# A fused attention, mixture and mixing kernel on one Trainium2 core: six shared PSUM banks, a decode by masks, first-batch pooling on TensorE, and a new table of order keys

## The chip, the cores and the metric

The kernel runs on one NeuronCore of a Trainium2 chip. Five engines work side by side on it: TensorE (PE; its weight loads are shown as PEld), VectorE (DVE), ScalarE (ACT), GpSimd (POOL) and the queue that issues all DMAs (SP). The metric is device time in microseconds, the median of several runs of the whole program; lower is better.

## The reference

Eight batches, 576 tokens, model width 512, all in fp32. Three stages follow each other:

```python
k_p = k.reshape(B, H, 72, 8, 64).mean(axis=3)          # keys and values are pooled by eight
v_p = v.reshape(B, H, 72, 8, 64).mean(axis=3)
attn = softmax(q @ k_p.T / 8);  x = attn @ v_p         # 8 heads, joined to 512 columns
logits = x @ w_gate                                    # 4 experts, the best 2 are weighted by softmax
for e in range(4):                                     # each expert: causal attention with head size 64
    a = softmax(causal(x @ wq[e] @ (x @ wk[e]).T / 8))
    out += gate[e] * (a @ (x @ wv[e]) @ wo[e])
theta = out @ w_theta
y = w_tok_r @ (out * cos(theta)) + w_tok_i @ (out * sin(theta))
u = out + y
result = u + max(u @ w_ch, 0)
```

The weights `w_theta`, `w_tok_r`, `w_tok_i` and `w_ch` reach the kernel as 64-bit floating point words, so it makes fp32 out of two 32-bit halves itself (here called the decode).

## The kernel before

Almost every product is made from a high and a low part of each factor (`mm3`: high by high, low by high, high by low), so one logical product is three matmuls into one PSUM bank, and every result is evicted twice: ACT copies the high part, and DVE or POOL subtracts it from the value to get the low part.

**Stages.** In the first stage, per batch: keys and values are pooled (`pool_kv`), queries meet pooled keys 128 tokens at a time (`attn_half`: scores, maximum, exponential, normalisation, transposes, product with the values), then the projections to expert queries and keys (`proj_qk`, two pairs of experts `p`) and values and gate logits (`proj_v`), and the experts' causal attention (`moe`, calling `scores`, `norm`, `turn`, `heads`). The expert keys `kh` are copied by DMA to the other half of the partitions before `scores` may read them. While this runs, 26 pieces of `w_theta` and `w_tok` are decoded (`decode_to`) and put into DRAM as high and low parts; eight pieces of `w_ch` are decoded later. The second stage, per batch: `mix` makes `out`, theta, sine and cosine, and `tokens` makes the two large products and the result. The first `mix` stands beside the last batch of the first stage.

**Order.** Nothing is issued in the order written. `Plan` records every operation, gives each a key (a start and a length per part of the program in `PARTS`, lines 43 to 55, plus a shift per engine and tile name in `SHIFT`, lines 56 to 96), and `issue` lists them greedily: the operation that its own cost rules let start first, and among equals that with the lowest key. The rules are estimates in the code (`price`, `LAT`, `DMA_LAT`); the result is one fixed order for each engine and for SP, and every engine waits in that order.

**Names and lines that the change touches.** PSUM has eight banks: two named `t` for transposes, two named `acc` for accumulations, four named `s` for scores and for `mix`. `decode` (lines 687 to 704) uses three ACT instructions, two DVE instructions and one POOL product to make the value, then ACT and POOL to split it. `pool_kv` (lines 736 to 777) adds eight slices in three steps on POOL, in the first batch partly on DVE (`on`, `FIRST_DVE`, line 28); ACT writes the two halves of the block-diagonal tiles `kbd` and `vbd`. `WHOLE` (line 26) names the 128-token tiles whose exponential is taken in one ACT instruction over eight heads after a DVE addition of the maximum, instead of eight ACT instructions with a sum each. In `mix` (lines 1105 to 1153) DVE and ACT share the range reduction of theta.

```python
A.activation(s, hi_w.bitcast(F32), AF.Copy, bias=FLUSH)
V.tensor_scalar(t, hi_w, 3, 0x40000000, op0=OP.logical_shift_left, op1=OP.bitwise_xor)
V.scalar_tensor_tensor(t, lo_w, 29, t, op0=OP.logical_shift_right, op1=OP.bitwise_or)
A.activation(s, s, AF.Sign, bias=flush)
A.activation(t.bitcast(F32), t.bitcast(F32), AF.Abs)
P.tensor_tensor(s, s, t.bitcast(F32), op=OP.mult)
```

Of the kernel before, what the change touches and what calls it, by code (L numbers as in the profile page):

```python
# [20 lines left out]
S = 576  # L21
# [4 lines left out]
WHOLE = {1, 2, 3, 4}, {0}  # L26

FIRST_DVE = {"k0", "k2", "pm0", "v0", "vr", "vrb0", "w0", "w3", "w4", "w6"}
# [15 lines left out]
    "first": (-1302.83, 63.19), "kv first": (-249.24, 366.9), "attn first 0": (-2208.92, 30.55),  # L44
    "attn first 1": (-552.72, 6.54), "proj_v first 0": (-1145.19, 56.03), "proj_qk0 first 0": (-185.37, 1302.94),
# [3 lines left out]
    "moe1": (29.54, 22.32), "decode": (150.23, 0.58), "wp": (-141.08, 3.51), "loadc first": (-6.04, 1083.14),  # L49
    "wtok first": (-212.16, 3987.86), "moe1 last": (27.48, 103.73), "mix first": (770.4, 161.1),  # L50
    "wtok": (2281.89, 4299.31), "wch": (-794.95, 122.81), "loadc": (-901.73, 22508671.56), "tokens": (85.02, 33.36),
    "mix": (85.18, 31.94), "constants first": (-1492.94, 5143.97), "clear first": (-2169.17, 8594480.35),
    "weights first": (-1120.91, 244.57), "load 1": (-21.92, 2656.27), "load first k": (-1565.62, 16.63),
    "load first q": (-1211.16, 0.84), "load first v": (-1596.57, 239.37),
}
SHIFT = {
    "ACT.G": 310.7, "ACT.G*": -60.8, "ACT.chs": 547.28, "ACT.d_hi": 469.68, "ACT.d_raw": -47.45, "ACT.d_s": 807.39,
    "ACT.gates": 299.94, "ACT.gates*": 299.58, "ACT.kbd": -11.49, "ACT.kbd*": -340.09, "ACT.kh": -2.28,
    "ACT.kh*": 65.35, "ACT.pa": -42.54, "ACT.pa*": 44.32, "ACT.pev": 4.6, "ACT.pev*": -912.36, "ACT.pod": -26.03,
# [137 lines left out]
class Plan:  # L197
# [107 lines left out]
    def price(eng, method, outs, ins, args, kw):  # L305
# [18 lines left out]
        if eng == "POOL":  # L324
            if method == "tensor_scalar":
                return n / 1.2 + 310
            if method == "tensor_tensor":
                return 1001.0 if n == 512 else 2.12 * n + 140
# [143 lines left out]
def body(ctx: ExitStack, tc, qT, kT, vm, vr, wqk, wvg, wo, woT, wth, wtok, wch, out):  # L472
# [50 lines left out]
    def on(b, what):  # L523

        return V if b == 0 and what in FIRST_DVE else P

# [736 lines left out]
```

## Time and profile before

| | |
|---|---|
| Three runs | 980.51, 982.76, 984.83 us (median 982.76) |
| The profiled execution | 980.56 us, its span 978.8 us |
| Busy in the span | PE 916.0, PEld 858.5, ACT 650.3, DVE 600.0, POOL 516.7 us |
| The chain that ended last | PE 64%, ACT 17%, DVE 8%, DMA 4%, POOL 3% of the span |
| First matmul | 12.28 us |
| The first stage ends | about 553 us, where TensorE begins its first long row of token products |

Busy time of PE counts a matmul from its issue to its modelled end, so a PE that reads nearly full can still be held up. The stretches matter more than the mean: the first stage (33 to 465 us) keeps four engines busy, the passage to the second stage (465 to 553 us) has gaps, and the rest is one row of matmuls.

### The profile page before, as it was taken

The page shows a single profiled execution, that of the slowest core. Times are in us where ns is not written, and L with a number is a line of the kernel's source. Part 1 is how long each engine was busy: PE and PEld are TensorE (multiplying, and loading weights), DVE is VectorE, ACT ScalarE, POOL GpSimd, SP SyncE. Part 2 cuts the span into 40 slices and gives each one's busy share as a digit, 9 for nine tenths or more (in the row PEclk, how much of TensorE's full clock was granted, in tenths as well). Part 3 has the DMA queues.
Part 4 walks back from the last instruction along what each step waited for, and adds up shares of the span by engine and source line. Part 5 has one row for each costly group of instructions (what it writes and reads, how often), then busy time and mean ns, then how long its engine had stood idle before and what let it go on. Part 6 is the DMA issues. An engine that isn't in the chain of part 4 may idle for free.

```text
span 978.8 us, 19095 instructions
## 1 busy us (share of the span) xinstructions
PE 916.0 (94%) x6384; PEld 858.5 (88%) x6384; DVE 600.0 (61%) x1718; ACT 650.3 (66%) x2026; POOL 516.7 (53%) x693
## 2 busy tenths in 40 slices
PE   2888999999899999999888999999999999999998
PEld 2887988898889899988866799999999999999998
DVE  5877887787878788887756745272424534262412
ACT  4689989798888999987768864262535444363510
POOL 7877777577386755544355774261625335151420
PEclk9999999999999999999989999999999999999999
DMA  9444445335444433334277413020110202010001
GB/s 279 138 143 122 122 123 150 115 108 140 119 118 116 136 96 87 89 103 115 51 232 243 154 44 92 1 85 13 38 56 13 80 1 70 1 38 13 25 25 49
DMA packets 78434, 91.63 MB, mean 94 GB/s; under 512 B 11264, under 2 KB 60928, under 8 KB 78336
## 3 DMA queue, kind: packets, MB, share of 16 engines
q1 hardware_dynamic: 78336, 90.41, 31.4%
q8 instruction: 51, 0.84, 0.4%
q14 instruction: 47, 0.39, 0.1%
HBM read 58.34 MB, written 26.28 MB: 86 GB/s over the span
## 4 chain that ended last, share of the span: by engine, by line
PE 64%; ACT 17%; DVE 8%; DMA 4%; POOL 3%; issue 3%; SPq 1%; POOLq 0%; ACTq 0%; DVEq 0%
PE acc L466 46%; PE s L466 14%; PE t L466 4%; ACT pp L466 4%; ACT pt L466 2%; DMA kh<-kh 2%; ACT pev L466 2%; ACT qs L466 1%; DVE s L466 1%; ACT kh L466 1%; ACT pa L466 1%; DVE pa L466 1%; DMA qraw<-in_qT_dram 1%; ACT xT L466 1%; DVE kl L466 1%
## 5 line engine op out<-in xcount | busy, mean ns | idle before, releaser
L466 PE MATMUL acc<-toks,z 128*128 128x288 f32 x1536 | 242.3, 297 | 2.0 <-ACT z L466 1.0
L466 PEld LDWEIGHTS acc<-toks,z 128*128 128x128 f32 x1536 | 223.9, 188 | 9.5 <-POOL z L466 1.8
L466 POOL TENSOR_TENSOR us<-u,us 128x288 fp32r<-128x288 f32 x64 | 51.9, 811 | 198.4 <-ACT us L466 198.3
L466 PE MATMUL acc<-xT,wqs 128*128 128x256 f32 (+1 forms) x768 | 123.3, 303 | 3.4 <-DVE logit L466 1.4
L466 PE MATMUL acc<-us,chs 128*128 128x288 f32 x768 | 114.1, 297 | 0.6 <-DVE o L466 0.5
L466 PEld LDWEIGHTS acc<-xT,wqs 128*128 128x128 f32 x768 | 106.4, 189 | 7.5 <-PE acc L466 3.4
L466 PEld LDWEIGHTS acc<-us,chs 128*128 128x128 f32 x768 | 107.9, 188 | 5.0 <-DVE o L466 1.5
L466 DVE TENSOR_TENSOR u<-acc,xt 128x288 f32<-128x288 f32 x64 | 29.1, 455 | 132.4 <-PE acc L466 132.4
L466 ACT CAST us<-u 128x288 fp32r<-128x288 f32 x64 | 27.6, 431 | 120.6 <-DVE u L466 120.5
L466 POOL TENSOR_TENSOR z<-zf,z 128x512 fp32r<-128x512 f32 x64 | 81.9, 1298 | 33.7 <-ACT z L466 33.6
L466 POOL TENSOR_SCALAR pev<-pev,lb,G 128x128 f32<-128x128 f32 (+4 forms) x80 | 52.5, 657 | 72.6 <-DVE lb L466 30.0
L466 DVE TENSOR_TENSOR pt<-t,pt 128x512 fp32r<-128x512 f32 (+4 forms) x160 | 75.7, 484 | 15.2 <-ACT pt L466 13.2
L466 ACT ACTIVATE pp<-s,mx 128x72 f32<-128x72 f32 x232 | 74.6, 336 | 6.6 <-DVE mx L466 6.0
L466 PE MATMUL acc<-wvs,xT 128*128 128x260 f32 x480 | 77.6, 292 | 1.2 <-DVE kl L466 0.4
L466 DVE CUSTOM_DVE_ANT_0 s<-s,mask 128x128 f32<-128x128 f32 (+2 forms) x144 | 69.6, 494 | 14.7 <-PE s L466 12.7
L466 ACT CAST pt<-t 128x512 fp32r<-128x512 f32 (+4 forms) x160 | 67.8, 437 | 13.8 <-PE t L466 12.9
L466 PE MATMUL s<-kbd,qraw 128*128 128x144 f32 x320 | 60.3, 311 | 16.2 <-DMA qraw<-in_qT_dram 12.3
L466 PE MATMUL acc<-pt,v 128*128 128x320 f32 (+4 forms) x416 | 68.1, 296 | 5.6 <-ACT yg L466 1.6
L466 PE MATMUL s<-kh,qs 128*128 128x128 f32 (+2 forms) x192 | 62.3, 355 | 10.3 <-DMA kh<-kh 8.0
L466 PEld LDWEIGHTS acc<-pt,v 128*128 128x128 f32 x416 | 60.7, 191 | 11.2 <-ACT yg L466 3.1
L466 PEld LDWEIGHTS acc<-wvs,xT 128*128 128x128 f32 x480 | 65.5, 189 | 4.0 <-ACT yg L466 0.8
L466 PE MATMUL s<-wos,ys 128*128 128x512 f32 x192 | 66.1, 402 | 0.4 <-DVE zf L466 0.3
(177 smaller groups left out, 2244.8 us busy)
## 6 DMA issues: line engine op xcount, KB each, us to landing
qraw<-in_qT_dram SPq DMA_DIRECT2D x40, 256.0 KB, 3.6
out_dram<-o SPq DMA_DIRECT2D x64, 144.0 KB, 1.8
kraw<-in_kT_dram SPq DMA_DIRECT2D x15, 576.0 KB, 4.1
yraw<-ygD SPq DMA_DIRECT2D x16, 512.0 KB, 4.3
vraw<-in_vm_dram SPq DMA_DIRECT2D x15, 512.0 KB, 4.1
d_raw<-in_wtok_dram SPq DMA_DIRECT2D x18, 288.0 KB, 2.9
toks<-tokD SPq DMA_DIRECT2D x18, 288.0 KB, 6.0
ygD<-yg SPq DMA_DIRECT2D x32, 160.0 KB, 2.9
```

The source lines that it names most:

```text
L466: o.ins = o.fn(*[a.real() if isinstance(a, View) else a for a in o.args], **{k: a.real() if isinstance(a, View) else a for k, a in o.kw.it ...
```

## The change

Accumulators and scores take their banks from one ring of six (`bank`, named `s`), with the two transpose banks as they were. The decode no longer uses ACT to make the value: four DVE instructions make a 0/1 factor and the bits, into a tile `d_t` of its own, and both parts leave by one DMA instead of two. The first batch's keys and values are summed over their eight slices by TensorE (eight matmuls with the identity into one bank) and written to `kbd` and `vbd` from PSUM with a 0/1 mask per half (`half`, `half64`); in later batches POOL writes both halves of `kbd` with the mask, and ACT and POOL write `vbd` whole, without the clearing of these tiles at the start. The remainder values `vr` keep high and low part in one tile, and `pq`, `pr` carry the rest of the probabilities in both halves of the partitions. Token tile 2 of batches 1 to 7 joins `WHOLE`. The weight splits of the start go from DVE to POOL (`FIRST_DVE`). In `mix`, two steps change places between ACT and DVE, and the first batch's absolute value goes to DVE. The planner prices a change of the operands' base partition (`TURN`), a longer DMA latency and slower copies inside SBUF, keys last-batch parts separately, and has new numbers in `PARTS` and `SHIFT`.

```diff
-WHOLE = {1, 2, 3, 4}, {0}
-FIRST_DVE = {"k0", "k2", "pm0", "v0", "vr", "vrb0", "w0", "w3", "w4", "w6"}
+WHOLE = {1, 2, 3, 4}, {0, 2}
+FIRST_DVE = {"pm0"}
...
-    "proj_v": (25.85, 26.92), "moe0": (-65.19, 3.47), "moe0 last": (-448.84, 0.5), "proj_qk0": (37.95, 13.99),
+    "proj_qk1": (2.55, 7.6), "attn": (-25.47, 25.84), "proj_v": (38.41, 19.54), "moe0": (-61.92, 1.9),
...
+    TURN = 118.0
+
-    DMA_ISSUE, DMA_LAT, DMA_RATE, DMA_ALL, DMA_SLOT, RELEASE = 600.0, 1300.0, 184.0, 262.0, 150.0, 130.0
+    DMA_ISSUE, DMA_LAT, DMA_RATE, DMA_ALL, DMA_SLOT, RELEASE = 600.0, 1700.0, 184.0, 262.0, 150.0, 130.0
...
+    def bank():
+
+        return ps.tile([128, 512], F32, name="s", bufs=6)
...
-        A.activation(s, hi_w.bitcast(F32), AF.Copy, bias=FLUSH)
-        V.tensor_scalar(t, hi_w, 3, 0x40000000, op0=OP.logical_shift_left, op1=OP.bitwise_xor)
+        V.tensor_scalar(s, hi_w.bitcast(F32), FLUSH, FLUSH, op0=OP.add, op1=OP.not_equal)
+
+        V.tensor_scalar(t, hi_w, 3, 0x3FFFFFFF, op0=OP.logical_shift_left, op1=OP.bitwise_and)
         V.scalar_tensor_tensor(t, lo_w, 29, t, op0=OP.logical_shift_right, op1=OP.bitwise_or)
-        A.activation(s, s, AF.Sign, bias=flush)
-        A.activation(t.bitcast(F32), t.bitcast(F32), AF.Abs)
+        V.scalar_tensor_tensor(t, hi_w, -0x40000000, t, op0=OP.bitwise_and, op1=OP.bitwise_or)
         P.tensor_tensor(s, s, t.bitcast(F32), op=OP.mult)
...
     def pool_kv(b):
         kt, q, v0, v1 = ld[b]
+        def summed(raw, n, k):
+
+            pl.lane = "pool"
+            acc = bank()[:, :n * k]
+            for r in range(8):
+                T.matmul(acc, ident, raw[:, :, r], start=r == 0, stop=r == 7)
+            return acc.rearrange("d (p k) -> d p k", k=k)[:, :, None, :]
+
+        X = P
         for p, n, raw in kt:
-            X = on(b, f"k{p}")
+            if b == 0:
+                V.tensor_tensor(kbd[:, p_], summed(raw, n, 72).to_broadcast([128, n, 2, 72]),
+                                half64[:, None, :, None].to_broadcast([128, n, 2, 72]), op=OP.mult)
+                continue
...
-            for e in range(2):
-                s_ = slice(64 * e, 64 * e + 64)
-                A.activation(kbd[s_, p:p + n, e], t[s_, :, 0], AF.Copy, scale=1.0 / 64)
+            X.tensor_tensor(kbd[:, p_], t[:, :, 0:1].to_broadcast([128, 2, 2, 72]),
+                            half64[:, None, :, None].to_broadcast([128, 2, 2, 72]), op=OP.mult)
...
-                s_ = ps.tile([128, 512], F32, name="s", bufs=4)[:, :288]
+                s_ = bank()[:, :288]
...
-                acc = ps.tile([128, 512], F32, name="acc")
+                acc = bank()
...
-            V.tensor_scalar(th[:m], pth[:m], INV2PI, MAGIC, op0=OP.mult, op1=OP.add)
-            A.activation(th[:m], th[:m], AF.Copy, bias=-MAGIC)
+            A.activation(th[:m], pth[:m], AF.Copy, bias=MAGIC, scale=INV2PI)
+            V.tensor_scalar(th[:m], th[:m], -MAGIC, None, op0=OP.add)
...
-            A.activation(th[:m], r[:m], AF.Abs)
+            if b == 0:
+                V.tensor_scalar(th[:m].bitcast(I32), r[:m].bitcast(I32), 0x7FFFFFFF, None, op0=OP.bitwise_and)
+            else:
+                A.activation(th[:m], r[:m], AF.Abs)
```

What the order makes of it is shown at three places. The first is TensorE's start. `kbd` and `qraw` are pooled keys and queries, `pm` and `pq` the normalised probabilities; in the changed kernel `kraw` and `pev` hold the first batch's raw keys, `vraw` and `pm` its raw values. Before:

```order
L466 MATMUL s<-kbd,qraw 128x144 x8
L466 MATMUL t<-ident,pm 128x128 x4
L466 MATMUL t<-ident,pq_177 128x128
L466 MATMUL s<-kbd,qraw 128x144 x4
L466 MATMUL t<-ident,pm 128x128 x4
```

and now:

```order
L486 MATMUL s<-kraw,ident 128x144 x8
L486 MATMUL s<-pev_145,ident 128x72 x8
L486 MATMUL s<-pev_163,ident 128x72 x5
L486 MATMUL s<-kbd,qraw 128x144 x3
L486 MATMUL s<-pev_163,ident 128x72 x3
L486 MATMUL s<-vraw,ident 128x128 x4
L486 MATMUL s<-kbd,qraw 128x144 x5
L486 MATMUL s<-vraw,ident 128x128 x4
L486 MATMUL s<-pm,ident 128x64 x13
L486 MATMUL t<-ident,pm 128x128 x4
```

Forty-five of the 48 pooling matmuls stand ahead of the first transposes.

The second place is a decode in the middle of the first stage. Before, ScalarE's list, where three of the rows between expert copies (`qs`, `kh`) and exponentials (`pev`, `pod`) are the decode's:

```order
L466 ACTIVATE qs_83<-acc 64x320
L466 ACTIVATE d_s<-d_raw 128x288
L466 ACTIVATE qs_83<-acc 64x256
L466 ACTIVATE d_s<-d_s,flush 128x288
L466 CAST pt_1154<-t 128x8x64
L466 CAST pt_1335<-t 64x128
L466 ACTIVATE pev_161,sum_118<-s,mxb 128x128
L466 ACTIVATE qs_83<-acc 64x64
L466 CAST kh_602<-acc 64x320 x2
L466 ACTIVATE d_raw<-d_raw 128x288
```

and now VectorE's list:

```order
L486 TENSOR_REDUCE mx<-s 128x4
L486 TENSOR_SCALAR d_t<-d_raw 128x288
L486 TENSOR_SCALAR d_s<-d_raw 128x288
L486 COPY logit_160<-s 128x4
L486 TENSOR_TENSOR pa_3538<-t,pa_3519 128x4x128
L486 TENSOR_TENSOR pr_3524<-t,pr_3514 128x128
L486 TENSOR_TENSOR v_3383<-s,v_3383 128x2x64
L486 TENSOR_TENSOR v_3390<-s,v_3390 128x2x64
L486 SCALAR_TENSOR_TENSOR d_t<-d_raw,d_t 128x288
L486 TENSOR_TENSOR pp_149<-s,mx 128x4x72
L486 SCALAR_TENSOR_TENSOR xT_3624<-s,xT_3614 128x256
L486 SCALAR_TENSOR_TENSOR d_t<-d_raw,d_t 128x288
```

The decode's instructions left ScalarE and stand, four instead of two, among the maxima and low parts of VectorE.

The third place is TensorE between an expert key tile and the first scores that read it, for the second pair of experts of batch 4 (`wqs` the projection weights, `kh1` the keys after their copy by DMA). Before, with buffer numbers:

```order
L466 MATMUL acc_5250<-xT01_3606,wqs0_353 128x256
L466 MATMUL t_5281<-ident_85,pm_5258 128x128 x4
L466 MATMUL s_5290<-kbd_87,qraw_4641 128x144 x2
L466 MATMUL t_5302<-ident_85,pev0_161 128x128 x4
L466 MATMUL s_5313<-kbd_87,qraw_4984 128x144 x2
L466 MATMUL t_5320<-ident_85,pev0_161 128x128
L466 MATMUL s_5322<-kh1_655,qs1_166 128x128
```

and now (the key tile `s_5057` ends 25 rows above the first row here; 23 more matmuls of 320 columns and four transposes stand between):

```order
L486 MATMUL s_5152<-xT11_3985,wqs0_362 128x320
L486 MATMUL s_5178<-kbd_208,qraw_4448 128x144 x2
L486 MATMUL s_5183<-kbd_208,qraw_4448 128x144
L486 MATMUL t_5190<-ident_95,pev0_145 128x128 x4
L486 MATMUL t_5196<-ident_95,pev0_145 128x128
L486 MATMUL s_5200<-kh1_727,qs1_101 128x128
```

The scores moved behind the projections of the second half, so more matmuls stand between a key tile and its first reader.

## Rows read from the trace of the kernel before

**Rows 1.** The page: busy time per engine, and the last chain by engine.

```profile
PE 916.0 (94%) x6384; PEld 858.5 (88%) x6384; DVE 600.0 (61%) x1718; ACT 650.3 (66%) x2026; POOL 516.7 (53%) x693
...
PE 64%; ACT 17%; DVE 8%; DMA 4%; POOL 3%; issue 3%; SPq 1%; POOLq 0%; ACTq 0%; DVEq 0%
```

**Rows 2.** Three stretches: length, busy us (instructions) of PE, PEld, DVE, ACT, POOL, PEclk, DMA share, GB/s.

```profile
33.00:465.00 432.00, 404.59 (x2945) 377.95 (x2945) 346.27 (x1190) 380.07 (x1459) 283.24 (x441) 0.99 0.42 118
465.00:553.00 88.00, 75.77 (x433) 63.35 (x432) 58.37 (x154) 68.56 (x170) 44.92 (x51) 0.96 0.58 178
553.00:979.00 426.00, 422.19 (x2942) 405.13 (x2940) 174.14 (x304) 186.05 (x348) 163.33 (x148) 1.00 0.13 39
```

**Rows 3.** Waits of TensorE over the span: us in total, times, longest.

```profile
PE s L466 <- DMA kh<-kh: 8.0, 7, 2.4
...
PE acc L466 <- ACT yg L466: 3.2, 7, 0.7
...
PE acc L466 <- DVE logit L466: 2.5, 8, 1.1
```

**Rows 4.** ScalarE by tile: ns min/median/max, first and last start us.

```profile
L466 ACT ACTIVATE d_s<-d_raw x34: 421/462/541, 19.6 to 587.6; 128x288 f32<-128x288 f32 x18, 128x256 f32<-128x256 f32 x16
L466 ACT ACTIVATE d_s<-d_s,flush x34: 492/529/626, 21.7 to 588.6; 128x288 f32<-128x288 f32 x18, 128x256 f32<-128x256 f32 x16
L466 ACT ACTIVATE d_raw<-d_raw x34: 433/460/522, 44.2 to 591.3; 128x288 f32<-128x288 f32 x18, 128x256 f32<-128x256 f32 x16
L466 ACT ACTIVATE kbd<-kt x34: 258/322/352, 8.9 to 359.7; 64x144 f32<-64x144 f32 x30, 64x72 f32<-64x72 f32 x4
L466 ACT ACTIVATE pp<-pp x11: 672/685/688, 21.1 to 371.7; 128x576 f32<-128x576 f32 x11
L466 ACT ACTIVATE th<-r x36: 614/633/662, 521.2 to 925.3; 128x512 f32<-128x512 f32 x36
```

**Rows 5.** ScalarE, groups by form: busy us, mean ns, idle before and what ended it.

```profile
L466 ACT ACTIVATE pp<-s,mx 128x72 f32<-128x72 f32 x232 | 74.6, 336 | 6.6 <-DVE mx L466 6.0
```

**Rows 6.** VectorE by tile.

```profile
L466 DVE TENSOR_SCALAR d_raw<-d_raw x34: 254/310/2429, 43.2 to 588.4; 128x288 int32<-128x288 int32 x18, 128x256 int32<-128x256 int32 x16
L466 DVE SCALAR_TENSOR_TENSOR d_raw<-d_raw x34: 407/450/1034, 43.8 to 590.8; 128x288 int32<-128x288 int32 x18, 128x256 int32<-128x256 int32 x16
L466 DVE TENSOR_TENSOR pp<-s,mx x22: 441/448/458, 20.2 to 371.3; 128x288 f32<-128x288 f32 x22
L466 DVE TENSOR_REDUCE l<-pp x11: 745/753/761, 22.1 to 373.2; 128x8 f32<-128x584 f32 x11
```

**Rows 7.** GpSimd, groups by form.

```profile
L466 POOL TENSOR_TENSOR kt<-kt 128x288 f32<-128x288 f32 x14 | 11.3, 808 | 0.4
L466 POOL TENSOR_TENSOR vrb<-vrh,hm 128x512 fp32r<-128x512 f32 x7 | 7.3, 1047 | 2.9 <-PE acc L466 2.7
```

**Rows 8.** VectorE and GpSimd in order of time, 586 to 592 us: start, length.

```profile
588.35 2.43 DVE L466 TENSOR_SCALAR d_raw<-d_raw 128x256 int32<-128x256 int32 x1
...
588.22 2.41 POOL L466 TENSOR_TENSOR ys<-yraw,ys 128x1024 fp32r<-128x1024 f32 x1
```

**Rows 9.** The stretch of the first mix, columns as in group 2.

```profile
530.00:550.00 20.00, 15.31 (x71) 10.48 (x69) 12.66 (x21) 19.25 (x39) 12.51 (x11) 1.00 0.72 244
```

**Rows 10.** VectorE in order of time, at the first batch's keys.

```profile
6.93 0.76 DVE L466 TENSOR_TENSOR kt<-kraw 128x576 f32<-128x576 f32 x1 [0.26 <-DMA kraw<-in_kT_dram]
```

**Rows 11.** TensorE in order of time, 12 to 33 us.

```profile
12.28 1.78 PE L466 MATMUL s<-kbd,qraw 128*128 128x144 f32 x6 [12.28 <-DMA qraw<-in_qT_dram]
17.05 2.77 PE L466 MATMUL s<-kbd,qraw 128*128 128x144 f32 x10 [2.99 <-ACT kbd L466]
...
31.85 1.14 PE L466 MATMUL s<-kbd,qraw 128*128 128x144 f32 x8
...
32.95 0.39 PE L466 MATMUL acc<-wvs,xT 128*128 128x260 f32 x1
```

**Rows 12.** The stretch that group 11 spans, columns as in group 2.

```profile
12.28:32.95 20.67, 13.43 (x71) 11.99 (x71) 14.53 (x34) 11.93 (x42) 17.04 (x27) 1.00 0.81 256
```

More of the change, by code (lines that the diff above doesn't have):

```diff
@@ L183 @@
 class Op:
-    __slots__ = ("eng", "fn", "args", "kw", "cost", "deps", "users", "key", "left", "ready", "roots", "start", "end", "n", "ins", "method", "lane", "load", "part", "kind", "soft", "port", "bytes", "seq")
+    __slots__ = ("eng", "fn", "args", "kw", "cost", "deps", "users", "key", "left", "ready", "roots", "start", "end", "n", "ins", "method", "lane", "load", "part", "kind", "soft", "base", "port", "bytes", "seq")
 class Engine:
@@ L285, in add @@
         o.bytes = outs[0].box.size * outs[0].box.itemsize if outs else ins[0].box.size * ins[0].box.itemsize if ins else 0
+        o.base = self.base(eng, outs, ins)
+        if eng == "DMA" and all(isinstance(a, View) and not a.root.pool.dram for a in args[:2]):
+            o.bytes *= 1.7
         o.port = self.shares(eng, method, outs, ins, kw)
@@ L302, in shares, with base @@
         return len(sb) > 1 and (outs[0].root.psum or method in ("tensor_tensor", "scalar_tensor_tensor"))
+    @staticmethod
+    def base(eng, outs, ins):
+        if eng not in ("DVE", "ACT", "POOL"):
+            return ()
+        return tuple((a.box.__array_interface__["data"][0] - a.root.base) // a.root.row
+                     for a in outs[:1] + (ins if eng != "ACT" else []))
     @staticmethod
@@ L607, in body @@
                         channel_multiplier=-1)
+    half = aw.tile([128, 2], F32, name="half")
+    half64 = aw.tile([128, 2], F32, name="half64")
+    for t, x in ((half, 1.0), (half64, 1.0 / 64)):
+        V.memset(t, 0.0)
+        for e in range(2):
+            V.memset(t[64 * e:64 * e + 64, e:e + 1], x)
     before = keep.tile([128, 4, 4], F32, name="before")
@@ L758, in attn_half @@
         pa = [awork.tile([128, 4, 320], F32R, name=f"pa{c}", bufs=1) for c in range(2)]
-        pr = awork.tile([128, 320], F32R, name="pr", bufs=1)
+        pr = [awork.tile([128, 320], F32R, name=f"pr{c}", bufs=1) for c in range(2)]
         for o, new in tiles:
@@ L820, in proj_qk @@
             for w in range(2):
-                acc = ps.tile([128, 512], F32, name="acc")
+                acc = bank()
                 c0 = 256 * p + 128 * w
@@ L854, in proj_v @@
             h, o = (0, 128 * t) if t < 2 else (1, min(128 * t, S - 128) - 256)
[L855 removed]
+            acc = bank()
             for kt in range(4):
@@ L915, in scores @@
         for c0, m in parts:
-            a = ps.tile([128, 512], F32, name="s", bufs=4)[:, :m]
+            a = bank()[:, :m]
             last = c0 + m == n
@@ L968, in heads @@
         for e in range(2):
-            acc = ps.tile([128, 512], F32, name="acc")
+            acc = bank()
             nj = 2 if h == 0 else 4
```

224 lines of the change are left out of this document (112 added, 112 removed), and 5 rows, old and new, of the table PARTS.

## Prediction, written before the changed kernel ran

> **What bounds the kernel now.** I read the page's totals first, then the stretches, then the waits of the engine that bounds, and last the operations that the change touches.
>
> TensorE is busy for 94% of the span, so it looks as if only fewer matmuls could help [rows 1]. The chain that ended last says otherwise: only 64% of it is TensorE's, 17% is ScalarE's, 8% VectorE's, 4% DMA, 3% GpSimd's. The stretches tell where [rows 2]. From 553 us on, TensorE is busy 422.2 of 426 us with 2942 instructions, one per 145 ns, and the other engines are below half: this part is matmuls alone, the change takes none away there, and I expect it to cost the same. From 33 to 465 us, nearly as many instructions (2945) take 432 us although many are shorter, and ScalarE is busy 88% of the time (380.1), VectorE 80% (346.3), GpSimd 66% (283.2). An engine at 88% that works in a fixed order and must wait for others has little room, so here ScalarE sets the pace with TensorE. From 465 to 553 us TensorE idles 12 of 88 us. Waits by name are few: 8.0 us for the DMA that copies expert keys, then 3.2 and 2.5 us for accumulator banks still being evicted [rows 3]. So the gain, if any, lies in the first 553 us, and comes from ScalarE, from key copies and from banks.
>
> **The change part by part.** The sum stands against the profiled execution's 980.56 us (span 978.8), which lies 0.2% under the median of the runs, 982.76.
>
> *ScalarE loses work.* Each decode loses three ACT instructions of 0.462, 0.529 and 0.460 us, 1.45 us [rows 4]; 28 of the 34 decodes stand ahead of 553 us (26 go to DRAM, two of the eight of `w_ch` stand in the first mix): 40.6 us. The 34 writes of `kbd` at 0.322 us go: 10.9 us [rows 4]. Seven token tiles join `WHOLE`: 56 short exponentials at 74.6 / 232 = 0.322 us go, 18.0 us, and seven of 0.685 us come, 4.8 us [rows 4, 5]: 13.2 us less. The first mix loses five absolute values of 0.633 us, 3.2 us [rows 4]. Together 67.9 us.
>
> *VectorE gains work.* Each decode gains one TENSOR_SCALAR and one SCALAR_TENSOR_TENSOR, priced at the medians of those it has, 0.310 and 0.450 us: 28 times 0.76 is 21.3 us [rows 6]. The seven tiles add 14 additions of 0.448 and seven reductions of 0.753 us: 11.6 us [rows 6]. Together 32.9 us. The exchange of the two theta steps I cost at nothing: one pass of 512 columns for another on either engine, and behind 553 us beside TensorE's row.
>
> *GpSimd gains work.* It writes `kbd` (14 instructions like the 288-column one of 0.808 us, 11.3 us) and makes the masked values (14 at most as long, 11.3 us), and loses seven `vrb` products of 1.047 us, 7.3 us [rows 7]: 15.3 us more.
>
> *What that is worth.* A microsecond on an engine costs what share of its work lies on the chain. For ScalarE that is 17% of 978.8 over 650.3 us, 0.26; for VectorE 0.13; for GpSimd 0.06 [rows 1]. So -67.9 x 0.26 + 32.9 x 0.13 + 15.3 x 0.06 = -12.5 us. That is one end: it holds if no other path is nearly as long. The other end goes by the heaviest engine: in the stretch of 432 us VectorE's 346.3 us become 377.7 us (26 decodes and the seven tiles), nearly ScalarE's present 380.1, so the stretch shrinks by 0.6%, 2.7 us [rows 2]. I take -8 us, the middle.
>
> *Key copies.* The waits of 8.0 us [rows 3] stand where scores follow their keys closely. In the third place shown of the order, 23 more matmuls of 320 columns stand between; at 145 ns each [rows 2] that is 3.3 us, more than the longest wait of 2.4. Between 0 and -8 us; I take -5, since copies are also queued on SP behind others.
>
> *Banks.* With one ring of six, an accumulation need not wait for the second-last one to be evicted while a score bank is free. The two named waits make 5.7 us [rows 3]; the eviction itself has to come anyway, and scores may now find accumulations in their banks, so between +2 and -6: I take -3.
>
> *The first mix.* From 530 to 550 us ScalarE is busy 19.25 of 20 us and TensorE has 71 instructions, half its usual number [rows 9]. There a microsecond of ScalarE counts nearly whole: two decodes and five absolute values, 6.1 us, of which 1.6 are counted above. But VectorE, at 12.7 of 20 us, takes much of it over. Between 0 and -4.5 us; I take -2.
>
> *The start.* TensorE began at 12.28 us, when the queries landed [rows 11]; now it begins when the first keys land, about 8 us: before, VectorE took them at 6.93 us [rows 10], and one 256 KB piece is now issued ahead of them. It pools with 48 matmuls of fp32, each two instructions. A 144-column instruction took 2.77 / 10 = 0.277 us at 17 us, and 1.14 / 8 = 0.143 us at 31.85 us [rows 11]; the profile gives the granted clock of the whole stretch as 1.00, the 2.4 GHz level [rows 12], so the row of the clock does not explain the factor of two. By columns the pooling is 16 instructions of 144, 32 of 72, 16 of 128 and 32 of 64: 16.7 us at the slow pace, 8.6 at the fast. The room is 4.3 us ahead of 12.28 and the 7.2 us that TensorE idles between there and the first value projection at 32.95 us (20.67 us less 13.43 busy [rows 12]); VectorE and GpSimd are freed of the first pooling, whose end TensorE awaited for 2.99 us [rows 11]. So this point moves by +5 to -4 us. I take -1.
>
> The Trainium skill says in "TensorE: Matmul & The Clock Gate" (Part 1) that the array's clock is throttled by default, to half, and that activity releases it. The fall from 0.277 to 0.143 us after the array had become busy agrees, though the row of the granted clock does not show it. By that rule an earlier start also ends the slow pace earlier, and the start would give 3 us rather than 1.
>
> *The sum:* -8 - 5 - 3 - 2 - 1 = -19, so 980.56 - 19 = **961.6 us**.
>
> **The rivals.**
>
> *More is won.* ScalarE's relief counts whole by the chain (-12.5), key copies and bank waits vanish (-8, -6), the mix gives 4.5 and the start 4: 946 us. For it speaks that TensorE's idle time is understated, since a busy TensorE is not one at its peak: 2945 instructions in 432 us. Against it, that VectorE comes to 87% of that stretch.
>
> *A wait takes the place of the one removed.* TensorE and ScalarE now wait for VectorE where VectorE waited for ScalarE; key copies and banks end the same way, since an evicted bank needs VectorE's low part too. Then only the 2.7 us of the heaviest engine are left: 978 us, no change that can be measured (for this kernel that is about 0.5%). For it speaks the third wait of TensorE, which is for VectorE [rows 3].
>
> *VectorE is locked out by GpSimd: slower.* At 588.35 us a decode TENSOR_SCALAR, of 0.310 us at the median, took 2.43 us; GpSimd's subtraction ran from 588.22 for 2.41 us, and VectorE ended within 0.2 us of it [rows 8]. The 52 added decode instructions from 33 to 465 us are of the two forms that show this (longest 2.43 and 1.03 us [rows 6]). The point from which it decides: VectorE passes ScalarE's present 380.1 us when the added ones take 22.2 / 52 = 0.43 us on the mean (346.3 and the tiles' 11.6 being fixed); the medians give 0.38. At 0.8 us VectorE has 399.5 us, at the same 88% a stretch of 454, 22 us more; less the 11 us of the other terms, 992 us. Against it: GpSimd is busy 66% of that stretch with pieces of about 1 us, and yet the medians are short.
>
> The Trainium skill's "GPSIMD Engine Reference" (section 1, Specifications) has it as a rule: GpSimd's SBUF interface is shared with VectorE, with contention from VectorE instructions in a two-port mode or with two SBUF inputs. The rows at 588 us agree. Taken as a rule for every added instruction, it speaks against this change and for the 992 us.
>
> *The change does not do what it says.* The order shows all accumulations in the common ring and no decode step left on ScalarE, so only the bank sharing can be void, if both kinds are always held; that is 964.6 us and within the forecast.
>
> **How the numbers follow.** The forecast of 961.6 us, with a range of its own of 952 to 972, gets 0.60; 946 gets 0.13; 978 gets 0.18; 992 gets 0.09. Faster by over 0.5% (under 977.9 us) are the first two and a third of the 978 case, 0.79; within 0.5% are the rest of that case, 0.12; slower 0.09. The range leaves out the 992 case and the lower half of the 946 case: 943 to 980 us.
>
> **What would show each step.** Right: ScalarE's busy time down by some 80 us over the span, VectorE's up by 25 to 40; between 33 and 465 us ScalarE near 75%, VectorE near 87%; TensorE's wait for key copies under 3 us; first matmul near 8 us and the first value projection at 28 to 37 us; the long token row beginning near 534 us and then 426 us to the end. Wrong would be: added decode instructions over 0.43 us on the mean, with TensorE waiting for VectorE in place of DMA and ScalarE; a first projection later than 37 us; or a second stage longer than 430 us, since its steps exchanged between ScalarE and VectorE are covered only by TensorE's row.

## The result, and the profile after

The changed kernel takes 967.85 us (median of four runs, 965.24 to 969.02) against 981.63 for the kernel before: ratio 0.9853, 95% interval 0.9818 to 0.9888, 14 us less. The forecast was 961.6 with a range of 943 to 980. The profiled execution has a span of 966.1 us; before it was 978.8.

The page after, busy time and the last chain by engine (they answer to [rows 1]):

```profile
PE 917.9 (95%) x6480; PEld 873.8 (90%) x6480; DVE 616.9 (64%) x1798; ACT 579.9 (60%) x1758; POOL 527.7 (55%) x683
...
PE 82%; DVE 6%; ACT 4%; POOL 4%; DMA 2%; issue 2%; SPq 0%; POOLq 0%; ACTq 0%; DVEq 0%
```

ScalarE lost 70 us of work and fell from 17% of the chain to 4%, VectorE gained 17. The same stretches as in [rows 2]:

```profile
33.00:465.00 432.00, 412.62 (x3059) 396.56 (x3059) 374.46 (x1285) 335.99 (x1257) 301.27 (x452) 0.97 0.42 120
465.00:553.00 88.00, 78.05 (x470) 68.03 (x469) 60.78 (x152) 59.83 (x144) 53.39 (x55) 0.96 0.58 186
```

In the first, TensorE has 114 instructions more than before; ScalarE is busy 78% instead of 88%, VectorE 87% instead of 80%. PEclk, the granted clock, is lower: 0.97 for 0.99. TensorE's waits (us, times, longest), for [rows 3]:

```profile
PE s L486 <- DMA kraw<-in_kT_dram: 8.3, 1, 8.3
PE s L486 <- issue: 4.4, 2, 2.4
PE s L486 <- DVE pt L486: 4.2, 5, 1.9
PE t L486 <- POOL pev L486: 4.2, 4, 1.4
PE s L486 <- POOL ys L486: 2.6, 2, 1.8
...
PE s L486 <- ACT yg L486: 1.1, 1, 1.1
...
PE s L486 <- DVE logit L486: 1.1, 2, 0.7
```

Key copies are gone from the list (8.0 us before), the two bank waits shrank from 5.7 to 2.2 us. VectorE's decode steps, for [rows 6], and then all that read `d_raw` from 33 to 465 us (busy us and count):

```profile
L486 DVE SCALAR_TENSOR_TENSOR d_t<-d_raw,d_t x68: 404/447/1489, 22.4 to 584.4; 128x288 int32<-128x288 int32 x36, 128x256 int32<-128x256 int32 x32
L486 DVE TENSOR_SCALAR d_t<-d_raw x34: 280/310/1554, 21.0 to 578.0; 128x288 int32<-128x288 int32 x18, 128x256 int32<-128x256 int32 x16
```
```profile
33.00:465.00 432.00, 43.51 (x101) 0.97 0.42 120
```

The medians are those of before; the mean of the 101 is 43.51 / 101 = 0.431 us.

**Where the time went.** Two marks cut the span: the gates of a batch (`gates<-logit`), and the first long row of token products. Each column is one profiled execution; in four other kernels below whose order at the start is the changed kernel's (decode on ScalarE, masks twice, theta back, idles filled), the gates of batch 0 stand at 55.95 to 58.17 us, so a difference of two or three us between single profiles says little.

| | before | after | change |
|---|---|---|---|
| to the gates of batch 0 | 61.46 | 58.71 | -2.8 |
| on to the gates of batch 7 | 406.98 | 399.51 | -7.5 |
| on to the long row (552.58, 533.08) | 84.14 | 74.86 | -9.3 |
| on to the end | 426.22 | 433.02 | +6.8 |

**What the sum did not have: the clock.** Granted clock times span says how much of TensorE's time is lost at most (idle time counts too): before (1 - 0.992) x 978.8 = 7.8 us, after (1 - 0.981) x 966.1 = 18.4 us. The falls stand behind idle places. Three pairs of stretches (TensorE alone: busy, PEclk, DMA share, GB/s), each an idle place and what follows:

```profile
27.40:32.60 5.20, 1.59 (x12) 0.88 0.76 251
32.60:38.60 6.00, 5.96 (x30) 0.53 0.17 45
83.00:88.00 5.00, 1.82 (x10) 0.80 0.64 176
88.00:93.00 5.00, 5.00 (x22) 0.52 0.44 154
150.00:155.00 5.00, 2.01 (x13) 0.93 0.72 224
155.00:162.00 7.00, 7.00 (x33) 0.57 0.01 2
```

After each, TensorE is busy nearly all the time at the lower of its two levels (0.5, 1.2 GHz) or close to it, so that "busy" is full while less work is done. Five matmuls of one kind take 2.50 us behind such a place and 1.43 us at 571.88 (shown further down):

```profile
526.88 2.50 PE L486 MATMUL s<-wps,ys 128*128 128x512 f32 x5 [1.79 <-POOL ys L486]
```

There are seven such places ahead of 533 us, at 31, 85, 154, 273, 386, 478 and 526 us; before there were three.

**The start.** TensorE in order of time (start, us):

```profile
16.87 0.78 PE L486 MATMUL s<-pev,ident 128*128 128x72 f32 x6
17.49 1.10 PE L486 MATMUL s<-vraw,ident 128*128 128x128 f32 x8
18.43 1.39 PE L486 MATMUL s<-kbd,qraw 128*128 128x144 f32 x10
...
27.39 0.38 PE L486 MATMUL s<-pa,vbd 128*128 128x256 f32 x1
30.21 1.22 PE L486 MATMUL s<-kbd,qraw 128*128 128x144 f32 x8 [2.44 <-issue]
32.64 0.80 PE L486 MATMUL s<-pa,vbd 128*128 128x256 f32 x2 [1.21 <-DVE vbd L486]
...
36.86 1.29 PE L486 MATMUL s<-wvs,xT 128*128 128x260 f32 x5
```

The first projection stands at 36.86 us, 3.9 later than before [rows 11]; in the four other kernels with this order at the start it stands at 34.67 to 36.20, so the delay is real, and 3.9 its largest size. Ten score matmuls took 1.39 us at 18.43, half the 2.77 of [rows 11]: the fast pace came early. Then TensorE idles twice, for 2.44 us for which the profile names no releaser ("issue"), and for 1.21 us for `vbd`. VectorE shows why the second: the low parts of `vbd`, whose high parts ScalarE had written by 26.34, stand in its order behind a sum that waited for ScalarE's exponential.

```profile
31.31 0.76 DVE L486 TENSOR_REDUCE l<-pp 128x8 f32<-128x584 f32 x1 [0.83 <-ACT pp L486]
31.98 1.37 DVE L486 SCALAR_TENSOR_TENSOR vbd<-s,half,vbd 128x128 fp32r<-128x128 f32 x6
```

### The profile page after: what moved, and what is told of

Same layout as the page of the kernel before. It is cut to its first block, busy times and chain, and to the rows that moved or that the text cites. A ratio compares the mean times of both kernels' runs of the same rounds, so it can differ in the third digit from the quotient of the medians.

```text
span 966.1 us, 19017 instructions
## 1 busy us (share of the span) xinstructions
PE 917.9 (95%) x6480; PEld 873.8 (90%) x6480; DVE 616.9 (64%) x1798; ACT 579.9 (60%) x1758; POOL 527.7 (55%) x683
## 4 chain that ended last, share of the span: by engine, by line
PE 82%; DVE 6%; ACT 4%; POOL 4%; DMA 2%; issue 2%; SPq 0%; POOLq 0%; ACTq 0%; DVEq 0%
PE s L486 75%; PE t L486 7%; POOL kv L486 1%; DVE mx L486 1%; DVE pt L486 1%; DVE l L486 1%; DMA kraw<-in_kT_dram 1%; DVE s L486 1%; ACT pev L486 1%; POOL pm L486 1%; DMA ygD<-yg 1%; ACT pt L486 0%; POOL ys L486 0%; DVE d_t L486 0%; ACT pp L486 0%
## 5 line engine op out<-in xcount | busy, mean ns | idle before, releaser
L486 PE MATMUL s<-toks,z 128*128 128x288 f32 x1536 | 216.3, 295 | 0.5 <-POOL z L486 0.5
L486 PEld LDWEIGHTS s<-toks,z 128*128 128x128 f32 x1536 | 208.2, 188 | 1.6 <-POOL z L486 0.8
L486 PE MATMUL s<-xT,wqs 128*128 128x256 f32 (+1 forms) x768 | 119.7, 300 | 0.0
L486 PE MATMUL s<-us,chs 128*128 128x288 f32 x768 | 110.1, 297 | 0.0
L486 PEld LDWEIGHTS s<-us,chs 128*128 128x128 f32 x768 | 105.6, 188 | 2.6 <-DVE zf L486 0.3
L486 PEld LDWEIGHTS s<-xT,wqs 128*128 128x128 f32 x768 | 105.3, 188 | 0.3
L486 PE MATMUL s<-pt,v 128*128 128x320 f32 (+4 forms) x416 | 72.3, 301 | 9.4 <-DVE pt L486 4.2
L486 PE MATMUL s<-wvs,xT 128*128 128x260 f32 x480 | 79.9, 300 | 0.8 <-DVE logit L486 0.7
L486 PEld LDWEIGHTS s<-pt,v 128*128 128x128 f32 x416 | 62.6, 195 | 14.2 <-DVE pt L486 5.6
L486 PEld LDWEIGHTS s<-wvs,xT 128*128 128x128 f32 x480 | 66.5, 194 | 1.8 <-PE s L486 0.9
```

What stands on the lines that cost most here:

```text
L486: o.ins = o.fn(*[a.real() if isinstance(a, View) else a for a in o.args], **{k: a.real() if isinstance(a, View) else a for k, a in o.kw.it ...
```

## The experiments

Where "the order is kept", every engine's list is the one of the kernel it starts from, but for the operation named: the planner lists an operation under its old engine and another is issued in its place, or the list is changed after planning. Each ran in five rounds beside the kernel before.

| Kernel | Start from | us | ratio to before, 95% interval |
|---|---|---|---|
| decode steps on ScalarE again | after | 976.96 | 0.9960 (0.9944 to 0.9977) |
| mask steps twice | after | 987.44 | 1.0068 (1.0041 to 1.0094) |
| six banks alone, listed anew | before | 997.46 | 1.0170 (1.0144 to 1.0197) |
| DMA estimates alone, listed anew | before | 995.57 | 1.0158 (1.0131 to 1.0185) |
| six banks, order kept | before | 976.88 | 0.9964 (0.9944 to 0.9985) |
| banks apart, listed anew | after | 1041.31 | 1.0618 (1.0602 to 1.0633) |
| theta steps back | after | 971.16 | 0.9898 (0.9877 to 0.9919) |
| `vbd` early | after | 961.45 | 0.9804 (0.9784 to 0.9824) |
| idles filled | after | 957.51 | 0.9763 (0.9745 to 0.9780) |
| `vbd` early, idles filled | after | 954.93 | 0.9731 (0.9699 to 0.9764) |
| `vbd` early, first pooling on VectorE | after | 975.59 | 0.9951 (0.9932 to 0.9969) |
| tile 2 by heads, on the 954.93 one | after | 965.57 | 0.9853 (0.9824 to 0.9882) |

**Decode steps back on ScalarE; mask steps twice.** `signs` issues a copy and a sign on ScalarE, `absolute` an absolute value.

```diff
-        V.tensor_scalar(s, hi_w.bitcast(F32), FLUSH, FLUSH, op0=OP.add, op1=OP.not_equal)
-        V.tensor_scalar(t, hi_w, 3, 0x3FFFFFFF, op0=OP.logical_shift_left, op1=OP.bitwise_and)
+        pl.add("DVE", signs, "tensor_scalar", (s, hi_w.bitcast(F32), FLUSH, FLUSH), ...)
+        V.tensor_scalar(t, hi_w, 3, 0x40000000, op0=OP.logical_shift_left, op1=OP.bitwise_xor)
...
-        V.scalar_tensor_tensor(t, hi_w, -0x40000000, t, op0=OP.bitwise_and, op1=OP.bitwise_or)
+        pl.add("DVE", absolute, "scalar_tensor_tensor", (t, hi_w, -0x40000000, t), ...)
```

> The changed kernel with two of the decode's four VectorE steps executed on ScalarE again, as three instructions (copy, sign, absolute value), in the places where the changed order has them; everything else keeps the order of the changed kernel (median 967.9 us). ScalarE gets back 34 x 1.45 = 49 us, 41 of it ahead of 553 us, VectorE loses some 28. My theory (ScalarE's relief is worth 8 us for 68 us of work, as the sum of the prediction had it) expects 41 x 0.12 = 5 us more, 973 us. Rival one (the gain came from key copies, banks and order, and ScalarE has slack at 78% of the stretch): within 2 us of 967.9. Rival two (ScalarE was most of it): 980 us or more, nearly the kernel before.

In the other, both SCALAR_TENSOR_TENSOR instructions are issued twice.

> The changed kernel with each of the two mask steps (SCALAR_TENSOR_TENSOR) of all 34 decodes executed twice, which changes no value; order kept. VectorE gets 68 x 0.50 = 34 us more, 27 ahead of the long token row, and would be busy some 93% of the stretch 33 to 465 us instead of 87%. My theory (TensorE and VectorE bound the first stage together now) expects 4 to 10 us more, 972 to 978 us. Rival one (VectorE has slack everywhere, its waits are not the ones that end last): within 2 us of 967.9. Rival two (VectorE is the bound of the first stage): 20 us or more, 988 us.

From the gates of batch 0 to those of batch 7 (columns as in [rows 2]): the changed kernel, then the decode on ScalarE,

```profile
58.71:458.22 399.51, 380.13 (x2817) 364.14 (x2817) 347.30 (x1205) 315.33 (x1188) 277.95 (x420) 0.97 0.42 120
```
```profile
57.53:468.27 410.74, 384.92 (x2816) 362.93 (x2816) 334.76 (x1158) 342.08 (x1257) 277.22 (x420) 0.98 0.42 116
```

and the masks twice:

```profile
58.17:472.95 414.78, 384.38 (x2815) 362.15 (x2814) 370.06 (x1252) 317.10 (x1187) 279.30 (x421) 0.98 0.41 115
```

Nearly all the loss lies in this stretch (of the 17.7 us between the profiled spans with the masks twice, 15.3). VectorE's 22.8 us more (370.06 - 347.30) cost 15.3: 0.67 per us. ScalarE's 26.8 us more, with 12.5 less on VectorE, cost 11.2; if VectorE counts 0.67, ScalarE counts (11.2 + 8.4) / 26.8 = 0.73. The expected 973 us and 972 to 978 were too low: 977.0 lies between my theory and its rival (980 or more), and 987.4 at the edge of its rival (20 us or more, 988). Work added to either engine cost about two thirds of its length, so neither alone was the bound. ScalarE's 0.73 also holds whatever the hand-overs between engines cost that the three steps now need; no run separates them.

**Banks.** The planner still sees two rings; the tiles are taken from one of six.

> The kernel before with every engine's order kept, but with the banks of accumulators and scores given out of one ring of six. The term of the prediction for banks alone: TensorE's waits for yg and logit (5.7 us) shrink to 2 us or less and the time by 1 to 4 us, 977 to 980 us against about 980.7. What the runs so far say (ScalarE is busy 89% of the time between the gates of batches 0 and 7 in the kernel before and sets its pace, so a bank that is free earlier is filled by nothing): within 1.5 us of the kernel before. Rival (banks are the source of the gain): 8 us less or more.

```diff
+    def bank(name, bufs):
+        t = ps.tile([128, 512], F32, name=name, bufs=bufs)
+        t.root.name, t.root.alias, t.root.given = "s", name, 6
+        return t
```

3.6 us less than before (980.47 in that comparison): the prediction's term. TensorE's first two waits there:

```profile
PE s L467 <- DMA qraw<-in_qT_dram: 12.0, 1, 12.0
PE s L467 <- DMA kh<-kh: 10.8, 8, 2.5
```

The waits for `yg` and `logit` are gone from the list's top, and those for key copies grew from 8.0 to 10.8 us; that part of what a free bank gave is handed to the next wait is a reading of this. My other expectation, under 1.5 us, missed for the whole kernel, but between the gates only 1.0 us is won, and 1.7 in the passage to the second stage:

```profile
61.10:467.10 406.00, 377.60 (x2776) 356.29 (x2774) 328.05 (x1130) 361.46 (x1391) 259.22 (x405) 0.98 0.42 117
```

The two kernels that were listed anew suffered at places for which the numbers were not made:

> The kernel before with one ring of six banks for accumulators and scores, and nothing else of the change; its planner lists the order anew with the old numbers. The banks' term of the prediction expects 1 to 5 us less than before (ratio 0.995 to 0.999), with TensorE's waits for yg and logit (5.7 us before) at 2 us or less. Rival one (scores now find accumulations in their banks, or the old numbers do not suit the ring): no gain or a loss of up to 5 us. Rival two (the ring is the main source of the gain): 10 us less.

> The changed kernel with two banks for accumulators and four for scores again; its planner lists the order anew with the new numbers. The total can suffer at the passages, so the pace of the first stage is compared: the last gates of batches 0 and 7 stand at 58.7 and 458.2 us in the changed kernel, 399.5 us apart; in the kernel before 407.0 apart; in the kernel before with six banks 398.7 apart. If banks are the source of the first stage's gain (not the 3 us of the prediction), the distance here is 405 to 412 us, and the total 975 us or more. Rival (the decode and the numbers are the source): 398 to 402 us, total within 3 us.

Six banks alone, listed anew, came to 997 us, outside all three expectations; waits stand at the passage to the second stage, 10.3 us for `ths`. Its stretch between the gates is 398.7 us, as short as the changed kernel's, which looks like the banks' work; but it holds 19 decodes where the kernel before has 25, and ScalarE's share is the same in both:

```profile
58.30:457.04 398.74, 377.38 (x2793) 355.75 (x2792) 325.93 (x1124) 354.68 (x1387) 251.81 (x399) 0.99 0.41 112
```
```profile
61.46:468.44 406.98, 381.57 (x2778) 356.42 (x2777) 327.98 (x1130) 362.18 (x1393) 259.69 (x405) 0.99 0.41 116
```

354.68 / 398.74 and 362.18 / 406.98 are both 0.890 (first row: six banks; second: before), and so is 361.46 / 406.00 with the order kept. That ScalarE set that pace, with either banks, is read from these shares. With the banks apart in the changed kernel the gates stand 441.6 us apart (73.70 to 515.35), beyond both expectations, and TensorE waits for accumulators instead, foremost:

```profile
PE acc L486 <- DVE kl L486: 17.2, 11, 4.2
PE acc L486 <- DVE qs L486: 13.0, 14, 3.0
```

The new numbers lean on the common ring; how much of the 73 us is the banks and how much a list made for others, this run does not say.

**DMA estimates alone.**

> The kernel before with the planner's new estimates for DMA alone (1700 in place of 1300 for the latency, copies inside SBUF 1.7 times as long), old numbers otherwise. If the key copies' waits were only the planner's error, TensorE's wait for them falls from 8.0 us to under 3 and the time by 2 to 8 us. Rival: the later scores leave the same hole for another wait, and the time stays within 2 us, or grows, since the old numbers were tuned for the old estimates.

The waits for key copies vanished from the list, and the time grew by 15 us: 416.6 us between the gates, with `yg`, `xT`, `kl` and `qs` in their place among the waits. The rival holds: the wait's going is by itself no gain.

**The start.**

```diff
+        early = [o for o in order if o.kind == "DVE.vbd" and o.part[0] == "kv first"]
+        order = [o for o in order if o not in early]
+        for o in early:
+            order.insert(1 + max(i for i, m in enumerate(order) if m in o.deps), o)
```

> The changed kernel with six VectorE instructions of the start (the low parts of vbd, which stood at 31.98 us behind other work) moved forward in VectorE's order to just behind what they need; every other order kept. My theory of the start (it is late, 36.9 us at the first value projection instead of the 32.95 before, because TensorE idles from 27.8 to 32.6 us for these, and its granted clock then falls to 0.5 until 39 us) expects the first projection at 31 to 33 us, no fall of the clock there, and 3 to 6 us less in all, 962 to 965 us. Rival (the next batch sets the pace, the start is hidden): the first projection comes earlier, the time stays within 2 us of 967.9.

TensorE in order of time in this kernel:

```profile
26.71 0.38 PE L490 MATMUL s<-pa,vbd 128*128 128x256 f32 x1
26.93 1.14 PE L490 MATMUL s<-kbd,qraw 128*128 128x144 f32 x8
27.81 0.49 PE L490 MATMUL s<-pa,vbd 128*128 128x256 f32 x2
...
32.65 1.08 PE L490 MATMUL s<-wvs,xT 128*128 128x260 f32 x5 [1.71 <-DVE xT L490]
```

The idle of 2.44 us and the fall of the clock are gone, the first projection is 4.2 us earlier in these two profiles, and the kernel 6.4 us faster by the medians, a little more than expected. By the ratios it is 4.8 us, with intervals that just touch. That the start is hidden by what follows, the rival, is out.

> The kernel with vbd's low parts early (961.5 us, first value projection at 32.65 us), and the first batch's keys and values summed by six VectorE reductions into the same banks instead of 48 TensorE matmuls; order kept otherwise. VectorE is idle until 12.5 us there; 4352 elements at the pace of its other reductions (584 in 0.756 us) are 5.6 us. Theory one (TensorE's pooling costs the start time, 15 us of matmuls of which most run at half pace): kbd is ready by 14 us instead of 18 and the first projection comes at 28 to 31 us, the time 2 to 4 us less. Theory two (TensorE's early work is what makes it run at full pace from 18 us on): scores at half pace longer, first projection at 32 to 36 us, the time the same or up to 3 us more.

This trial does not answer its question. Its reductions stand where the last of eight matmuls stood, while the loads of the weights into the same tiles wait only for the first four; so they came behind those loads (VectorE idles 7.1 us for one, until 18.47), and the first batch's sums are in part of weights. As a start that is 10.7 us later (43.34 for 32.65) it cost 14.1 us, which agrees with a start that counts in full.

**The clock.**

```diff
+WARM = {
+    1391: (8, 256),
+    753: (12, 256),
...
+}
...
+            if o.n in WARM:
+                for _ in range(WARM[o.n][0]):
+                    self.idle(t[:, :256], 256, o.kw.get("start", True))
```

> The changed kernel with 111 matmuls of zeros put into eleven of TensorE's idle places (84 to 88, 151 to 155, 272, 384, 475 and 523 to 527 us), each writing zeros ahead of, or adding zeros to, the bank that the next matmul writes; orders kept. In the changed kernel the granted clock fell to 0.5 behind these idles for 24 us in all, which is 12 us of TensorE's time at full clock. Theory (the falls of the clock are real losses, since TensorE is on the chain for 82%): mean granted clock over 0.99 instead of 0.981 and 6 to 12 us less, 956 to 962 us. Rival one (other engines set the pace there, and TensorE catches up): clock up, time within 2 us. Rival two (the zeros do not keep the clock): clock as before, and 0 to 5 us more, since they stand in the way of what comes next.

(There are 110 of them.) TensorE from 83 to 88 us in this kernel:

```profile
83.26 1.19 PE L541 MATMUL s<-idle 128*128 128x256 f32 x8
84.64 0.76 PE L506 MATMUL s<-kbd,qraw 128*128 128x144 f32 x4 [0.18 <-POOL kbd L506]
85.14 1.68 PE L541 MATMUL t<-idle 128*128 128x256 f32 x12
87.01 0.66 PE L506 MATMUL t<-ident,pm 128*128 128x128 f32 x4 [0.19 <-POOL pm L506]
```

and the stretches between the gates and from 84 to 94 us, columns as in [rows 2]:

```profile
57.86:450.05 392.19, 381.42 (x2895) 365.52 (x2895) 346.34 (x1205) 315.14 (x1188) 278.24 (x421) 1.00 0.44 122
84.00:94.00 10.00, 9.53 (x71) 8.74 (x71) 7.36 (x24) 7.87 (x35) 9.40 (x14) 1.00 0.46 147
```

The mean granted clock is 0.995, the stretch between the gates 392.2 us instead of 399.5, and the kernel 10.3 us faster (8.8 by the ratios, whose intervals lie apart) with more work: theory, as expected. The falls of the clock are real losses.

> Both edits that made the changed kernel faster: vbd's low parts early (6 us) and the idle places filled with matmuls of zeros (10 us), the same 111 at the same places of the order. If both are the clock and the start, they add, since the start's fall of the clock (3.4 us) was not among those filled: 950 to 953 us, mean granted clock 0.995 or more. Rival (moving the start shifts the idles, so that zeros stand in the way and other falls come): 955 to 960 us.

954.93 us is the lowest median here, faster than both kernels; it is 2.6 less than with the idles filled alone, but these two intervals overlap. The gains add at most in part, nearer the rival: falls remain at 33, 470 and 562 us. The one at 33 us stands behind the same wait of 1.71 us ahead of the first projection that was followed by no fall in the kernel with `vbd` early alone, so the length of that wait did not decide it:

```profile
33.77 1.45 PE L510 MATMUL s<-wvs,xT 128*128 128x260 f32 x5 [1.71 <-DVE xT L510]
```

**The exchanged steps of theta.**

> The changed kernel with the two exchanged steps of theta executed on their old engines (the product on VectorE from PSUM, the subtraction on ScalarE), in the same places of the order. The sum of the prediction costed the exchange at nothing. Theory one (behind 533 us all is covered by TensorE): within 1.5 us of 967.9. Theory two (VectorE's step, now on SBUF alone, is held up by GpSimd at 565 to 572 us, 2.4 us for two where the mean is 0.65 each, and TensorE idles 1.8 us there): 1 to 3 us less, with that idle gone. Rival: 1 to 4 us more, since ScalarE at the first mix is the heavier engine.

971.16 us, 3.3 more, in size the rival's; the intervals of the two ratios just overlap. In its profile the passage from the last gates to the long row is 78.9 us at a PEclk of 0.89, in the changed kernel's 74.9 at 0.95, so the clock can account for it. Theory two is out: in the changed kernel there is a place where VectorE's new step is held up (two took 2.38 us), and TensorE idles nearby,

```profile
565.73 2.38 DVE L486 TENSOR_SCALAR th<-th 128x512 f32<-128x512 f32 x2
...
571.88 1.43 PE L486 MATMUL s<-wps,ys 128*128 128x512 f32 x5 [0.82 <-POOL ys L486]
```

but the exchange is not what the second stage lost by: from the long row on, this kernel takes 434.0 us.

**The third token tile head by head.** ScalarE's four exponentials are issued where VectorE's addition stood, and the sum is taken over their sums.

```diff
-                    V.tensor_tensor(pp[:, 4 * c:4 * c + 4, :72], sv, mx[...], op=OP.add)
+                    pl.add("DVE", four if single else nc.vector.tensor_tensor, "tensor_tensor", (pp[...], sv, mx[...]), ...)
```

> The fastest kernel so far (954.9 us, vbd early and idles filled), with the third token tile of batches 1 to 7 taken head by head again, as before the change: VectorE loses 14 additions of 0.447 and seven sums of 0.756 us for seven of 0.16, 10.4 us less; ScalarE gets 56 short exponentials for seven of 0.69 us, some 12 us more; places in the order kept. Theory one (VectorE, busy 88% between the gates of batches 0 and 7, alone sets the pace now, at the 0.7 us per us that the doubled masks showed): 7 us less, 946 to 950 us. Theory two (both engines count alike now: the decode put back on ScalarE cost 11 us in that stretch although VectorE lost 12.5 us of work, which at 0.7 each makes 27 us of ScalarE worth 20): 1 to 3 us more, 955 to 958 us. Theory three (the sums of the prediction, ScalarE 0.12 per us): 5 us less from VectorE, 1.5 more from ScalarE, 951 us.

965.57 us, 10.6 more: theory two in direction, and beyond its size. Between the gates, where all of it lies, ScalarE gained 12.0 us and VectorE lost 7.5 (first row: early `vbd` and filled idles; second: this one):

```profile
56.69:449.37 392.68, 381.59 (x2896) 365.62 (x2895) 346.52 (x1205) 315.28 (x1188) 277.73 (x421) 1.00 0.43 122
56.31:459.65 403.34, 386.88 (x2896) 367.84 (x2895) 339.02 (x1191) 327.25 (x1293) 278.89 (x420) 1.00 0.42 119
```

At 0.73 and 0.67 that is 3.7 us, so these prices do not carry over to another change. The rest may be the tile's longer way, eight exponentials in an order made for one; that was not separated.

## Why the prediction was right, point by point

The number was right; the sum behind it was not. A gain that was sized too small and losses that it did not have nearly cancelled: with `vbd` early and the idles filled, which the sum did not foresee, the kernel is 25.5 us faster than before (980.47 in that comparison) where the sum has 19. That the forecast came within 0.7% is in part luck.

*The engines (-8).* This is the term that the runs point at as mis-sized. From 33 to 465 us the busy shares came as forecast (ScalarE 78% and VectorE 87%, for 75% and 87%); over the span ScalarE lost 70 us (some 80 named) and VectorE gained 17, less than the 25 to 40 named. But a microsecond was priced by the chain's shares, 0.26 and 0.13, and the runs with the order kept show more: putting the decode back cost 9 us and the third tile 10.6 (on another base), where these shares give 7.8 and 1.9, and work added to the changed kernel cost 0.73 and 0.67 per us. For the decode, ScalarE's gain and VectorE's loss, both priced too low, nearly cancel; for the tile they do not. None of these is the gain itself: an order made for one form has no places for the other, so going back can cost more than going forth gave. By the two prices the 67.9 us less and 32.9 more would be -27.5 us, an estimate, not a run, and the same prices gave the tile a third of what it cost. A likely reason is that the chain names one of several ways that are nearly as long and does not say how soon the next one takes over; this was not shown by itself. The row that would have helped was ScalarE's 0.890 between the gates. VectorE, the heaviest engine afterwards, has 0.883 there with the idles filled and 0.892 with the masks twice. By equal shares 406.98 x 347.30 / 362.18 is 390 us, and with the clock kept it became 392.2. It is no law: with the decode back on ScalarE the two engines have 0.833 and 0.815, and with the third tile by heads 0.811 and 0.841.

*The new order keys (not in the sum).* What the new numbers in `PARTS` and `SHIFT` gave by themselves no run separates. With the old numbers, listing anew for six banks or for the new DMA estimates cost 17 and 15 us; with the new ones, listing anew for separate banks cost 73.

*Key copies (-5).* The wait went to zero, as expected; that this was worth 5 us is not shown. One kernel lost the waits and gained nothing (DMA estimates alone), another had more of them and was faster (six banks, order kept).

*Banks (-3).* 3.6 us with the order kept: right.

*The first mix (-2).* The passage from the last gates to the long row is 9.3 us shorter, and the row begins at 533.08 us (forecast 534). With the decode back on ScalarE the passage is the same 74.9 us, so the decode there is not the reason; six banks alone make it 1.7 shorter. The rest is open.

*The start (-1, +5 to -4).* It fell on the bad end, 36.86 us, inside the 28 to 37 named. The step that failed is the room, the 7.2 us that TensorE idled and that its pooling was to fill: what it waits for at 28 us is not its own pooling but VectorE's place for the low parts of `vbd`. Moving these forward gave 6.4 us (4.8 by the ratios). The Trainium skill's rule, "TensorE: Matmul & The Clock Gate" (Part 1), that the clock is throttled by default and activity releases it, would have made 3 us of the start. The 1.39 us at 18.43 agrees with it; the idle that follows took the gain back.

*The second stage (0).* 433.0 us, over the 430 named as wrong; in the other kernels with the changed second stage it is 431 to 434. So a term that was put at nothing is 5 to 8 us. TensorE is busy 3.6 us more there, with 14 more instructions; since the 96 that were added in all are the first batch's pooling, these are work that now stands behind the long row's beginning. It idles 1.8 us from 569 to 572 us, and 4.9 us pass from the last matmul to the end instead of 3.1; the last is of this one execution, as seven other kernels with this stage have 3.2 to 3.3. About half is thus bookkeeping between the stages, and what else lengthens it is open; with the theta steps put back it is no shorter (434.0).

*The clock (not in the sum).* By these counts 10.6 us more are lost than before; filling the idles gave 10.3 back. The prediction read the granted clock only where it asked about the start.

*The rivals.* Slower by VectorE's lock: the mean of the 101 decode steps is 0.431 us, at the 0.43 that was named as the point of decision for the added ones. But what that point stood for, VectorE's busy time passing 380.1 us, did not come (374.5), so the kernel did not meet this rival's condition. The longest step ends 0.14 us behind one of GpSimd:

```profile
570.42 1.55 DVE L486 TENSOR_SCALAR d_t<-d_raw 128x256 int32<-128x256 int32 x1
...
569.46 2.37 POOL L486 TENSOR_TENSOR ys<-yraw,ys 128x1024 fp32r<-128x1024 f32 x1 [0.38 <-ACT ys L486]
```

The Trainium skill's "GPSIMD Engine Reference" (section 1, Specifications), which has GpSimd's SBUF interface shared with VectorE, agrees with such steps, though no run shows in which of the modes that it names they run. The medians, which did not move, rule out that most of the added instructions suffer by it. That VectorE's wait takes the place of the one removed is partly so: `pt` 4.2 us, and two thirds of every added microsecond. More is won (946 us): the change as made did not come near it, and with its two losses mended it stands at 954.9.

## What to carry to other kernels

Price work that moves between engines by keeping the order and adding or removing some on the chip; shares of the last chain gave a third to a fifth of what added work cost here. Such a price holds for that change in that order; it missed the next one by a factor of three. Read the granted clock by stretches, not only its mean: behind the seven falls here the longest single wait was 1.1 to 2.4 us, and some matmuls of zeros into the bank that is written next bought about 1% of the kernel. When a planner's table is new, look for an operation that stands late for no reason at the passages; one such place cost 5 to 6 us, more than a ring of six banks gave.

## What was not expected of the hardware

- Behind idle places TensorE's granted clock falls to 0.5 while it is busy without a gap; seven falls in the changed kernel, at most 18.4 us lost in all. 110 matmuls of zeros of 256 columns hold it at 0.995.
- The row of the granted clock does not show the slow beginning: 1.00 where 26 instructions of 72 columns take 4.00 us at 12.24, and ten of 144 take 1.39 us at 18.43.
- VectorE's reduction of 1152 elements whose neighbours lie 288 bytes apart took 2.22 us, 1.9 ns each, into PSUM (in the kernel with the first pooling on VectorE); its sum over 584 adjacent ones into SBUF takes 0.753, 1.3 ns each [rows 6].
